# Loading the query weights and K first, and the gated unit's weights late, in a decode attention kernel

## The chip, the cores and the metric

The kernel runs on one core of a Trainium2 chip. The metric is device time in microseconds. The profile shows the engines PE (matrix products, with weight loads as PEld), DVE (vector), ACT (activations), POOL and SP, and 16 DMA engines that serve the queues of SP, ACT and POOL. In this kernel both SP and ACT issue the large loads, and ACT computes besides.

## The reference

One decoding step for 8 sequences with one token each. Two branches start from the normalized token and meet in a product.

```python
xn = _layernorm(x)                      # x: [8, 1, 512]
# branch A: attention over the last 2048 of 8192 cached keys; 32 query heads, 8 key heads, Dh 128
q = (xn @ wq)                           # wq: [512, 4096]
k = k_cache[:, :, Sk - W:, :]           # W = 2048, each key head serves 4 query heads
v = v_cache[:, :, Sk - W:, :]
p = softmax(q @ k.T * Dh ** -0.5)
s = (p @ v) @ wo                        # wo: [4096, 512]
# branch B: the gated unit
h = sigmoid(xn @ w_gate) * (xn @ w_up)  # [512, 1792] each
g = silu(h @ w_down)                    # w_down: [1792, 512]
out = x + s * g
```

All inputs are bf16. The windows of K and V are 32 MiB each, Wq and Wo 4 MiB each, the three weights of the gated unit 1.75 MiB each.

## The kernel before

**Tiles and the ring.** K and V are loaded in 16 tiles each of 2 MiB (one sequence, four of its eight key heads): K0 to K15 and V0 to V15. All large loads, weights too, go into a ring of 10 equal buffers (`ring_tile`, lines 90 and 91): a new tile takes the buffer of the tile ten allocations earlier, and its load waits until that one has been read. `free_bufs` counts in Python how many loads may be issued at a point of the program; `issue_loads` (line 133) issues from the sorted list `loads`. `load` (line 84) alternates between the queues of ACT and SP when no queue is given.

**Order of the start.** The program issues x, the three weights of the gated unit (`wg_sb`, `wu_sb`, `wd_sb`), the two halves of Wq, and then K and V as buffers allow. After the layer norm (lines 216 to 248) PE computes the gated unit (lines 251 to 285: 56 products with wg, 56 with wu, 28 with wd, to `gate`) and then the queries (`q_projection`, 128 products, and four copies into `qz_sb`).

**The slots.** The main loop (line 500) goes over slots t. A K or V tile is worked on in four slots. In slot t PE transposes a quarter of a K tile in two halves (`k_half`, line 321, each copied by DVE), multiplies the quarter of slot t - 1 with the queries (`qk`, line 335), and multiplies a quarter of V with the probabilities of slot u = t - 11 (`pv`, line 431). There are 64 such quarters, so t runs to 74. A batch takes eight slots. After a batch's scores its softmax is spread over slots by phase `ph` = t modulo 8: maximum at 0, `soft_exp` at 1 (a small product, a minimum, the exp on ACT, line 370), transposition and permutation at 2 (line 384 on DVE, line 390 on PE, copy on ACT at line 394), masks at 3 (line 402, DVE), denominators at 4 (`soft_den`, line 422). Each engine executes its own instructions in program order, DMA issues among them.

**The end.** Once all K and V loads are issued and seven buffers are free by count (slot 63), `load_wo` (line 458) issues Wo in seven pieces with a ring buffer each, four on SP and three on ACT. `o_rows(0)` and `o_rows(1)` turn the attention output around after the last slots of V, 64 products with Wo follow (line 541), then two DVE operations with `gate` and x, and two output DMAs. The PSUM buffer with the tag `misc` is single: the small product of `soft_exp`, the products with wd, the denominators and `o_rows` take turns in it.

Of the kernel before, what the change touches and what calls it, by code (L numbers as in the profile page):

```python
# [10 lines left out]
def kernel(  # L11
# [13 lines left out]
    nc = tc.nc  # L25
    P = 128
    B, _, D = A_x.shape
    _, Hkv, Sk, Dh = A_k_cache.shape
# [3 lines left out]
    F = B_w_gate.shape[1]  # L32
    KT = D // P
    FT = F // P
    win0 = Sk - W
    scale = float(Dh) ** -0.5
    HG = Hq // 4
# [7 lines left out]
    NJ = 4  # L45
# [4 lines left out]
    NT = B * NG  # L50
    SPB = NG * NJ
    NSLOT = B * SPB
    PV_LAG = SPB + 3
    QPAD = XR - rep
    RING = 10
    NCOL = 2
    DC = D // NCOL

    bf16 = mybir.dt.bfloat16
    f32 = mybir.dt.float32  # L60
    AF = mybir.ActivationFunctionType
    ALU = mybir.AluOpType
# [5 lines left out]
    work = ctx.enter_context(tc.tile_pool(name="work", bufs=1))  # L68
# [4 lines left out]
    psum = ctx.enter_context(  # L73
        tc.tile_pool(name="psum", bufs=2, space=bass.MemoryType.PSUM)
    )
    psum1 = ctx.enter_context(
        tc.tile_pool(name="psum1", bufs=1, space=bass.MemoryType.PSUM)
    )
# [5 lines left out]
    def load(dst, src, q=None):  # L84
        if q is None:
            q = queues[turn[0] % 2]
            turn[0] += 1
        q.dma_start(out=dst, in_=src)

    def ring_tile(shape, name):  # L90
        return ring.tile(shape, bf16, name=name, tag="ring", align_bytes=ALIGN)
# [1 line left out]
    x_bf = work.tile([B, D], bf16, name="x_bf")  # L93
    nc.sync.dma_start(out=x_bf[:], in_=A_x.flatten_outer_dims())

    wg_sb = ring_tile([P, KT, F], "wg_sb")
    wu_sb = ring_tile([P, KT, F], "wu_sb")
    wd_sb = ring_tile([P, FT, D], "wd_sb")
    load(wg_sb[:], B_w_gate.rearrange("(p kt) n -> p kt n", kt=KT), nc.scalar)
    load(wu_sb[:], B_w_up.rearrange("(p kt) n -> p kt n", kt=KT), nc.sync)  # L100
    load(wd_sb[:], B_w_down.rearrange("(p t) n -> p t n", t=FT), nc.sync)
    wq_view = A_wq.rearrange("(p kt) n -> p kt n", kt=KT)
    KH = KT // 2
    wq_sb = []
    for kh in range(2):
        t = ring_tile([P, KH, Hq * Dh], f"wq_sb{kh}")
        load(t[:], wq_view[:, kh * KH : (kh + 1) * KH, :], nc.scalar if kh == 0 else nc.sync)
        wq_sb.append(t)

    k_tiles = {}  # L110
    v_tiles = {}

    def load_kv(cache, i, name):
        b, gg = divmod(i, NG)
        t = ring_tile([P, CH, Dh], name)
        load(
            t[:].rearrange("p c d -> p (c d)"),
            cache[b, GL * gg : GL * (gg + 1), win0:Sk, :].rearrange(
                "j (p c) d -> p j (c d)", c=CH
            ),  # L120
        )
        return t

    loads = sorted(
        [(NJ * i, 0, i) for i in range(NT)]
        + [(NJ * i + PV_LAG, 1, i) for i in range(NT)]
    )
    loads_done = [0]  # L130
    free_bufs = [RING - 5]

    def issue_loads():
        while loads_done[0] < len(loads) and free_bufs[0] > 0:
            _, kind, i = loads[loads_done[0]]
            if kind:
                v_tiles[i] = load_kv(A_v_cache, i, "v_sb")
            else:
                k_tiles[i] = load_kv(A_k_cache, i, "k_sb")
            loads_done[0] += 1  # L140
            free_bufs[0] -= 1

# [3 lines left out]
    for j in range(NCOL):  # L146
        nc.gpsimd.dma_start(
            out=x2_sb[32 * j : 32 * j + B, :],
            in_=A_x.flatten_outer_dims()[:, DC * j : DC * (j + 1)],
# [7 lines left out]
    for off in range(-rep * (NJ - 1), rep * NJ, rep):  # L157
        nc.gpsimd.affine_select(
            out=SumM[:],
            in_=SumM[:],  # L160
# [9 lines left out]
        out=SumM_blk,  # L170
        in_=SumM_blk,
# [7 lines left out]
        out=SumM_blk,  # L179
        in_=SumM_blk,  # L180
# [11 lines left out]
        out=Jneg[:],  # L192
        in_=ident[:].rearrange("p (a j r) -> p j a r", j=NJ, r=rep),
        axis=AX.XY,
        op=ALU.add,
    )
    nc.vector.tensor_scalar(
        out=Jneg[:], in0=Jneg[:], scalar1=-scale, scalar2=None, op0=ALU.mult
# [4 lines left out]
        out=Hm[:],  # L203
        in_=ident[:].rearrange("p (a gl) -> p gl a", gl=GL),
        axis=AX.X,
        op=ALU.add,
# [4 lines left out]
        out=perm[:].rearrange("k (p gl) -> k p gl", gl=GL),  # L211
        in_=ident[:].rearrange("k (gl p) -> k p gl", gl=GL),
# [17 lines left out]
        out=rstd[:], in_=mv[:, 1:2], func=AF.Sqrt, bias=eps_t[:], scale=1.0  # L230
# [4 lines left out]
        out=xn_bf[:],  # L235
        in0=x_f[:],
# [6 lines left out]
    for kt in range(KT):  # L243
        nc.tensor.transpose(  # L244
            out=xnT_ps[:, kt, :], in_=xn_bf[:B, kt::KT], identity=ident[:B, :B]
# [2 lines left out]
    nc.vector.tensor_copy(out=xnT_sb[:], in_=xnT_ps[:])  # L248


    g_ps = psum.tile([P, FT, B], f32, name="g_ps", tag="s_ps")
    u_ps = psum.tile([P, FT, B], f32, name="u_ps", tag="s_ps")
    for w_sb, d_ps in ((wg_sb, g_ps), (wu_sb, u_ps)):
        for t in range(FT):
            for kt in range(KT):
                nc.tensor.matmul(
                    d_ps[:, t, :],
                    lhsT=w_sb[:, kt, t::FT],
                    rhs=xnT_sb[:, kt, :],
                    start=(kt == 0),  # L260
                    stop=(kt == KT - 1),
                )
    sig = work.tile([P, FT, B], f32, name="sig")
    nc.scalar.activation(out=sig[:], in_=g_ps[:], func=AF.Sigmoid)
    hT_sb = work.tile([P, FT, 32], bf16, name="hT_sb")
    nc.vector.memzero(hT_sb[:])
    nc.vector.tensor_tensor(
        out=hT_sb[:, :, :B], in0=sig[:], in1=u_ps[:], op=ALU.mult
    )
    b_ps = psum1.tile([NCOL * 32, DC], f32, name="b_ps", tag="misc")  # L270
    for t in range(FT):
        for j in range(NCOL):
            nc.tensor.matmul(
                b_ps[32 * j : 32 * (j + 1), :],
                lhsT=hT_sb[:, t, :],
                rhs=wd_sb[:, t, DC * j : DC * (j + 1)],
                start=(t == 0),
                stop=(t == FT - 1),
                tile_position=(0, 32 * j),
                skip_group_check=True,  # L280
            )
    sigb = work.tile([NCOL * 32, DC], f32, name="sigb")
    nc.scalar.activation(out=sigb[:], in_=b_ps[:], func=AF.Sigmoid)
    gate = work.tile([NCOL * 32, DC], f32, name="gate")
    nc.vector.tensor_tensor(out=gate[:], in0=sigb[:], in1=b_ps[:], op=ALU.mult)
    free_bufs[0] += 3
    issue_loads()


    def q_projection():  # L290
# [160 lines left out]
                op=ALU.mult,  # L451
            )


    wo_view = A_wo.rearrange("(hg p j) n -> p hg j n", p=P, j=4)
    wo_parts = {}

    def load_wo():
        for q, h0, h1, j0, j1 in (
            (nc.sync, 0, 2, 0, 4),  # L460
            (nc.scalar, 2, 4, 0, 4),
            (nc.sync, 4, 5, 0, 4),
            (nc.scalar, 5, 6, 0, 4),
            (nc.sync, 6, 7, 0, 4),
            (nc.scalar, 7, 8, 0, 2),
            (nc.sync, 7, 8, 2, 4),
        ):
            t = ring_tile([P, h1 - h0, j1 - j0, D], f"wo_sb{h0}{j0}")
            load(t[:], wo_view[:, h0:h1, j0:j1, :], q)
            for hg in range(h0, h1):  # L470
                for j in range(j0, j1):
                    wo_parts[hg, j] = t[:, hg - h0, j - j0, :]

    o2_sb = work.tile([P, HG, 4, 32], bf16, name="o2_sb")
    nc.vector.memzero(o2_sb[:])
    HGH = HG // NG
# [23 lines left out]
    for t in range(NSLOT + PV_LAG):  # L500
        u = t - PV_LAG
        b, ph = t // SPB - 1, t % SPB
        in_b = 0 <= b < B
        if t < NSLOT:
            k_half(t, 0)
        if in_b and ph == 3:
            soft_mask(b)
            dh_of[b] = soft_den_part(b)
        if t < NSLOT:
            k_half(t, 1)  # L510
        if in_b and ph == 2:
            soft_turn(b)
        if 0 <= t - 1 < NSLOT:
            qk(t - 1)
        if in_b and ph == 0:
            mj_of[b] = soft_max_part(b)
        if in_b and ph == 1:
            soft_exp(b, mj_of.pop(b))
        if u >= 0:
            pv(u)  # L520
        if in_b and ph == 2:
            soft_permute(b)
        if in_b and ph == 4:
            soft_den(b, dh_of.pop(b))
        if t < NSLOT and t % NJ == NJ - 1:
            free_bufs[0] += 1
        if u >= 0 and u % NJ == NJ - 1:
            free_bufs[0] += 1
        issue_loads()
        if loads_done[0] == len(loads) and not wo_parts and free_bufs[0] >= 7:  # L530
            load_wo()
        if u == NSLOT - NJ - 1:
            o_rows(0)
    o_rows(1)
# [4 lines left out]
    for n, (hg, j) in enumerate(order):  # L539
        for c in range(NCOL):  # L540
            nc.tensor.matmul(  # L541
                a_ps[32 * c : 32 * (c + 1), :],
                lhsT=o2_sb[:, hg, j, :],
                rhs=wo_parts[hg, j][:, DC * c : DC * (c + 1)],
                start=(n == 0),
                stop=(n == len(order) - 1),
                tile_position=(0, 32 * c),
                skip_group_check=True,
# [5 lines left out]
    for c in range(NCOL):  # L554
        queues[c].dma_start(
            out=out.flatten_outer_dims()[:, DC * c : DC * (c + 1)],
            in_=y_bf[32 * c : 32 * c + B, :],
# [31 lines left out]
```

## Time and profile before

| | |
|---|---|
| median of 3 runs | 206.28 us (205.15 to 206.87) |
| profiled execution, own time | 206.49 us |
| profiled execution, span | 204.4 us |
| PE busy | 158.1 us, 77% |
| PE weight loads | 117.0 us, 57% |
| DVE busy | 118.7 us, 58% |
| ACT busy | 15.7 us, 8% |
| DMA | 81.40 MB, mean 398 GB/s |
| chain that ended last | PE 43%, DMA 42%, DVE 11% |

The span goes from the first to the last instruction of the core; the execution's own time has some 2 us more around it. Times in views of the trace count from the start of the span. A timeline row has start, duration, engine, line, operation, output and input tile, shape and count; in brackets the idle time of the engine just before it and what ended that. PEclk is the granted share of PE's clock, in tenths. A row of ACTq or SPq is the issue of a DMA, not the transfer. A tile's name ends without its number, so `o_sb` stands for `o2_sb`, `x_sb` for `x2_sb`.

### The profile page before, as it was taken

What the parts mean: (1) busy time and instruction counts of PE and PEld (TensorE: products, weight loads), DVE (VectorE), ACT (ScalarE), POOL (GpSimd) and SP (SyncE); (2) the same over time, 40 slices, a digit from 0 to 9 for tenths busy, and PEclk for the clock granted to TensorE, in tenths of its full rate; (3) what the DMA queues carried; (4) which work ended last, traced back from release to release, by engine and by line L of the source; (5) the groups of instructions that cost most, each with busy time, mean ns of one, the idle gap of its engine ahead of it and who ended that gap; (6) DMA issues with size and microseconds to landing.
All of it is one profiled execution on the core that took longest, in us unless ns stands there. A gap on an engine that the chain in (4) does not pass through costs nothing.

```text
span 204.4 us, 5925 instructions
## 1 busy us (share of the span) xinstructions
PE 158.1 (77%) x2712; PEld 117.0 (57%) x2712; DVE 118.7 (58%) x248; ACT 15.7 (8%) x30; POOL 7.4 (4%) x20
## 2 busy tenths in 40 slices
PE   0003971999988997999899799988798996993893
PEld 0003941866656765676676577665666674662862
DVE  2402010367888687776868777686468767664311
ACT  0005000002020011002001100200020002002000
POOL 7600000000000000000000000000000000000000
PEclk9999997559999999999999999999799999997558
DMA  6999999999999999999999999999999999999700
GB/s 209 437 430 433 425 436 420 433 430 430 439 414 431 430 430 433 420 430 430 426 436 420 430 433 423 438 417 433 430 420 439 423 433 425 420 426 407 288 24 2
DMA packets 6728, 81.40 MB, mean 398 GB/s; under 512 B 776, under 2 KB 816, under 8 KB 1968
## 3 DMA queue, kind: packets, MB, share of 16 engines
q1 hardware_dynamic: 3472, 41.69, 47.9%
q10 hardware_dynamic: 3168, 39.33, 45.6%
q8 instruction: 21, 0.34, 0.6%
q14 instruction: 3, 0.02, 0.0%
q0 software_dynamic: 64, 0.01, 0.0%
HBM read 81.02 MB, written 0.01 MB: 396 GB/s over the span
## 4 chain that ended last, share of the span: by engine, by line
PE 43%; DMA 42%; DVE 11%; issue 1%; ACT 1%; SPq 1%; ACTq 0%
DMA v_sb<-in_A_v_cache_dram 19%; PE kT_ps L328 18%; DMA wq_sb<-in_A_wq_dram 16%; PE oT_ps L439 9%; PE s_ps L344 8%; DMA wo_sb<-in_A_wo_dram 7%; DVE kT_sb L331 5%; PE a_ps L541 3%; DVE pT_sb L402 3%; DVE pt_bf L384 2%; PE qT_ps L294 2%; PE pT_ps L390 1%; PE mb_ps L365 1%; PE den_ps L424 1%; DVE qz_sb L302 1%
## 5 line engine op out<-in xcount | busy, mean ns | idle before, releaser
L331 DVE COPY kT_sb<-kT_ps 128x1024 bf16<-128x1024 bf16 x128 | 83.3, 686 | 31.8 <-PE kT_ps L328 31.2
L328 PE MATMUL kT_ps<-ident,k_sb 128*128 128x128 bf16 x1024 | 71.4, 225 | 0.7 <-DVE kT_sb L331 0.7
L328 PEld LDWEIGHTS <-k_sb 128*128 128x128 bf16 x1024 | 62.3, 101 | 9.8 <-issue 8.8
L439 PEld LDWEIGHTS <-v_sb 128*128 128x128 bf16 x1024 | 31.1, 98 | 34.4 <-issue 26.3
L439 PE MATMUL oT_ps<-pT_sb,v_sb 128*128 128x16 bf16 x1024 | 34.9, 170 | 11.1 <-DVE pT_sb L402 6.8
L344 PE MATMUL s_ps<-kT_sb,qz_sb 128*32 128x512 bf16 x256 | 39.7, 610 | 0.0
L244 PE MATMUL xnT_ps<-ident,xn_bf 8*128 8x8 bf16 x4 | 0.3, 174 | 18.6 <-DVE xn_bf L234 18.6
L370 ACT ACTIVATE p_bf<-s_ps,nm 128x512 bf16<-128x512 f32 x8 | 5.5, 687 | 111.6 <-DVE nm L367 98.4
L244 PEld LDWEIGHTS <-xn_bf 8*128 8x128 bf16 x4 | 0.2, 114 | 18.5 <-DVE xn_bf L234 18.5
L344 PEld LDWEIGHTS <-qz_sb 128*32 128x32 bf16 x256 | 6.6, 93 | 6.9 <-issue 0.8
L402 DVE TENSOR_SCALAR pT_sb<-pc_bf,Hm 128x512 bf16<-128x512 bf16 x32 | 9.1, 346 | 1.2 <-ACT pc_bf L394 1.2
L294 PE MATMUL qT_ps<-xnT_sb,wq_sb 128*128 128x8 bf16 x128 | 3.7, 168 | 5.6 <-DMA wq_sb<-in_A_wq_dram 4.6
L294 PEld LDWEIGHTS <-wq_sb 128*128 128x128 bf16 x128 | 3.6, 104 | 6.0 <-DMA wq_sb<-in_A_wq_dram 4.7
L390 PE MATMUL pT_ps<-pt_bf,perm 128*128 128x512 bf16 x8 | 3.2, 402 | 5.0 <-DVE pt_bf L384 5.0
L541 PE MATMUL a_ps<-wo_sb,o_sb 128*32 128x256 bf16 x64 | 6.6, 386 | 0.2 <-issue 0.2
L232 DVE RECIPROCAL rstd<-rstd 8x1 f32<-8x1 f32 x1 | 0.1, 150 | 10.4 <-ACT rstd L229 10.4
L302 DVE CAST qz_sb<-qT_ps 128x64 bf16<-128x64 f32 x4 | 1.3, 586 | 8.4 <-PE qT_ps L294 8.4
L384 DVE STREAM_TRANSPOSE pt_bf<-p_bf 128x512 bf16<-128x512 bf16 x8 | 5.6, 702 | 0.9 <-ACT p_bf L370 0.9
L394 ACT CAST pc_bf<-pT_ps 128x512 bf16<-128x512 f32 x8 | 4.7, 586 | 16.3 <-PE pT_ps L390 16.3
L356 DVE TENSOR_REDUCE mx<-s_ps 128x1 f32<-128x512 f32 x8 | 5.5, 682 | 0.8 <-PE s_ps L344 0.8
L541 PEld LDWEIGHTS <-o_sb 128*32 128x32 bf16 x64 | 4.5, 136 | 2.0 <-issue 0.7
L426 DVE RECIPROCAL rden<-den_ps 128x32 f32<-128x32 f32 x8 | 2.9, 358 | 4.5 <-PE den_ps L424 4.5
(55 smaller groups left out, 62.6 us busy)
## 6 DMA issues: line engine op xcount, KB each, us to landing
k_sb<-in_A_k_cache_dram ACTq DMA_DIRECT2D x15, 2048.0 KB, 30.4
v_sb<-in_A_v_cache_dram SPq DMA_DIRECT2D x15, 2048.0 KB, 39.4
wq_sb<-in_A_wq_dram ACTq DMA_DIRECT2D x1, 2048.0 KB, 17.8
wq_sb<-in_A_wq_dram SPq DMA_DIRECT2D x1, 2048.0 KB
k_sb<-in_A_k_cache_dram SPq DMA_DIRECT2D x1, 2048.0 KB, 41.7
v_sb<-in_A_v_cache_dram ACTq DMA_DIRECT2D x1, 2048.0 KB, 36.3
wg_sb<-in_B_w_gate_dram ACTq DMA_DIRECT2D x1, 1792.0 KB, 9.1
wu_sb<-in_B_w_up_dram SPq DMA_DIRECT2D x1, 1792.0 KB, 14.3
```

The source lines that it names most:

```text
L294: nc.tensor.matmul(qT_ps[:, h * B : (h + 1) * B], lhsT=wq_sb[kt // KH][:, kt % KH, h * Dh : (h + 1) * Dh], rhs=xnT_sb[:, kt, :], start=(kt ...
L328: nc.tensor.transpose(out=kT_ps[:, jj, :], in_=k_sb[:, c0 + jj, :], identity=ident[:, :])
L331: nc.vector.tensor_copy(out=kT_tiles[t][:, h2 * HALF : (h2 + 1) * HALF, :], in_=kT_ps[:])
L344: nc.tensor.matmul(s_tiles[b][XR * gl : XR * (gl + 1), :], lhsT=qz_sb[:, b, GL * gg + gl, z0 : z0 + XR], rhs=kT[:, :, gl::GL], start=(x == 0),
L356: nc.vector.reduce_max(out=mx[:], in_=s_tiles[b][:], axis=AX.X)
L370: nc.scalar.activation(out=p_bf[:], in_=s_tiles.pop(b)[:], func=AF.Exp, bias=nm[:], scale=scale, accum_out=den128[:],)
L384: nc.vector.transpose(out=pt_bf[:], in_=p_bf[:])
L390: nc.tensor.matmul(pT_ps[:], lhsT=perm[:], rhs=pt_tiles.pop(b)[:], start=True, stop=True)
L394: nc.scalar.copy(out=pc_bf[:], in_=pT_ps[:])
L402: nc.vector.tensor_scalar(out=pT_tiles[b][:, :, gl].rearrange("p c x r -> p c (x r)"), in0=pc, scalar1=Hm[:, gl : gl + 1], scalar2=None, o ...
L439: nc.tensor.matmul(o_tiles[b][:, GW * gg : GW * (gg + 1)], lhsT=v_sb[:, CC * j + cc, :], rhs=pT_tiles[b][:, cc, :, x, :], start=(j == 0 an ...
L541: nc.tensor.matmul(a_ps[32 * c : 32 * (c + 1), :], lhsT=o2_sb[:, hg, j, :], rhs=wo_parts[hg, j][:, DC * c : DC * (c + 1)], start=(n == 0), ...
```

## The change

Wq's two halves become the first large loads, followed by K and V. The three weights of the gated unit come after K15 and V13, ahead of V14 and V15. Its products and activations move into the main loop: those with wg and wu, both with the multiply into `hT_sb`, to the end of slot 66 (behind the last batch's permutation), those with wd and `gate` to the end of slot 67. Their two PSUM tiles now use the tag `kT_ps`. Wo comes last, in two ring buffers of which the first is loaded by two DMAs and the second by five; they are part of the list of loads and so are issued when a buffer is counted free (slots 58 and 59). Queues alternate for all loads but the last piece of Wo, which goes to SP. All arithmetic stays as it was.

```diff
-    wg_sb = ring_tile([P, KT, F], "wg_sb")
-    wu_sb = ring_tile([P, KT, F], "wu_sb")
-    wd_sb = ring_tile([P, FT, D], "wd_sb")
-    load(wg_sb[:], B_w_gate.rearrange("(p kt) n -> p kt n", kt=KT), nc.scalar)
-    load(wu_sb[:], B_w_up.rearrange("(p kt) n -> p kt n", kt=KT), nc.sync)
-    load(wd_sb[:], B_w_down.rearrange("(p t) n -> p t n", t=FT), nc.sync)
...
-        load(t[:], wq_view[:, kh * KH : (kh + 1) * KH, :], nc.scalar if kh == 0 else nc.sync)
+        load(t[:], wq_view[:, kh * KH : (kh + 1) * KH, :])
...
+    def load_mlp(kind):
+        if kind == 2:
+            t = ring_tile([P, FT, D], "wd_sb")
+            load(t[:], B_w_down.rearrange("(p t) n -> p t n", t=FT))
+            wd_sb.append(t)
+        else:
+            t = ring_tile([P, KT, F], ("wg_sb", "wu_sb")[kind])
+            load(t[:], (B_w_gate, B_w_up)[kind].rearrange("(p kt) n -> p kt n", kt=KT))
+            (wg_sb, wu_sb)[kind].append(t)
...
+    loads[-2:-2] = [(2, 0), (2, 1), (2, 2)]
+    loads += [(3, 0), (3, 1)]
     loads_done = [0]
-    free_bufs = [RING - 5]
+    free_bufs = [RING - 2]
...
+    def load_wo(half):
+        t = ring_tile([P, HG // 2, 4, D], f"wo_sb{half}")
+        for h0, h1, j0, j1 in (
+            ((0, 2, 0, 4), (2, 4, 0, 4)),
+            ((4, 5, 0, 4), (5, 6, 0, 4), (6, 7, 0, 4), (7, 8, 0, 2), (7, 8, 2, 4)),
+        )[half]:
+            q = nc.sync if (h0, j0) == (7, 2) else None
+            o = half * (HG // 2)
+            load(t[:, h0 - o : h1 - o, j0:j1, :], wo_view[:, h0:h1, j0:j1, :], q)
...
-    g_ps = psum.tile([P, FT, B], f32, name="g_ps", tag="s_ps")
-    u_ps = psum.tile([P, FT, B], f32, name="u_ps", tag="s_ps")
-    for w_sb, d_ps in ((wg_sb, g_ps), (wu_sb, u_ps)):
+    def unit_in(w_sb):
+        d_ps = psum.tile([P, FT, B], f32, name="d_ps", tag="kT_ps")
...
+    def unit_mid():
+        g_ps, u_ps = d_tiles
+        sig = work.tile([P, FT, B], f32, name="sig")
+        nc.scalar.activation(out=sig[:], in_=g_ps[:], func=AF.Sigmoid)
+        nc.vector.tensor_tensor(
+            out=hT_sb[:, :, :B], in0=sig[:], in1=u_ps[:], op=ALU.mult
+        )
+
+    def unit_out():
+        b_ps = psum1.tile([NCOL * 32, DC], f32, name="b_ps", tag="misc")
...
-        if loads_done[0] == len(loads) and not wo_parts and free_bufs[0] >= 7:
-            load_wo()
+        if t == NSLOT + 2:
+            unit_in(wg_sb[0])
+            unit_in(wu_sb[0])
+            unit_mid()
+            free_bufs[0] += 2
+            issue_loads()
+        if t == NSLOT + 3:
+            unit_out()
+            free_bufs[0] += 1
+            issue_loads()
```

More of the change, by code (lines that the diff above doesn't have):

```diff
@@ L122, in load_kv @@
         return t
[L126 to L129, printed above, removed]
-    loads_done = [0]
-    free_bufs = [RING - 5]
+    wg_sb = []
+    wu_sb = []
+    wd_sb = []
+    def load_mlp(kind):
[7 more added lines that the diff above has]
+            (wg_sb, wu_sb)[kind].append(t)
+    loads = [
+        (kind, i)
+        for _, kind, i in sorted(
+            [(NJ * i, 0, i) for i in range(NT)]
+            + [(NJ * i + PV_LAG, 1, i) for i in range(NT)]
+        )
+    ]
+    loads[-2:-2] = [(2, 0), (2, 1), (2, 2)]
+    loads += [(3, 0), (3, 1)]
+    loads_done = [0]
+    free_bufs = [RING - 2]
+    wo_view = A_wo.rearrange("(hg p j) n -> p hg j n", p=P, j=4)
+    wo_parts = {}
+    def load_wo(half):
[7 more added lines that the diff above has]
+            load(t[:, h0 - o : h1 - o, j0:j1, :], wo_view[:, h0:h1, j0:j1, :], q)
+            for hg in range(h0, h1):
+                for j in range(j0, j1):
+                    wo_parts[hg, j] = t[:, hg - o, j, :]
     def issue_loads():
         while loads_done[0] < len(loads) and free_bufs[0] > 0:
-            _, kind, i = loads[loads_done[0]]
-            if kind:
+            kind, i = loads[loads_done[0]]
+            if kind == 0:
+                k_tiles[i] = load_kv(A_k_cache, i, "k_sb")
+            elif kind == 1:
                 v_tiles[i] = load_kv(A_v_cache, i, "v_sb")
+            elif kind == 2:
+                load_mlp(i)
             else:
-                k_tiles[i] = load_kv(A_k_cache, i, "k_sb")
+                load_wo(i)
             loads_done[0] += 1
@@ L248 @@
     nc.vector.tensor_copy(out=xnT_sb[:], in_=xnT_ps[:])
-    g_ps = psum.tile([P, FT, B], f32, name="g_ps", tag="s_ps")
-    u_ps = psum.tile([P, FT, B], f32, name="u_ps", tag="s_ps")
-    for w_sb, d_ps in ((wg_sb, g_ps), (wu_sb, u_ps)):
+    d_tiles = []
+    hT_sb = work.tile([P, FT, 32], bf16, name="hT_sb")
+    nc.vector.memzero(hT_sb[:])
+    gate = work.tile([NCOL * 32, DC], f32, name="gate")
+    def unit_in(w_sb):
+        d_ps = psum.tile([P, FT, B], f32, name="d_ps", tag="kT_ps")
         for t in range(FT):
@@ L262 @@
                 )
[L263 to L287, printed above, removed]
+        d_tiles.append(d_ps)
+    def unit_mid():
[4 more added lines that the diff above has]
+            out=hT_sb[:, :, :B], in0=sig[:], in1=u_ps[:], op=ALU.mult
+        )
+    def unit_out():
+        b_ps = psum1.tile([NCOL * 32, DC], f32, name="b_ps", tag="misc")
+        for t in range(FT):
+            for j in range(NCOL):
+                nc.tensor.matmul(
+                    b_ps[32 * j : 32 * (j + 1), :],
+                    lhsT=hT_sb[:, t, :],
+                    rhs=wd_sb[0][:, t, DC * j : DC * (j + 1)],
+                    start=(t == 0),
+                    stop=(t == FT - 1),
+                    tile_position=(0, 32 * j),
+                    skip_group_check=True,
+                )
+        sigb = work.tile([NCOL * 32, DC], f32, name="sigb")
+        nc.scalar.activation(out=sigb[:], in_=b_ps[:], func=AF.Sigmoid)
+        nc.vector.tensor_tensor(out=gate[:], in0=sigb[:], in1=b_ps[:], op=ALU.mult)
     def q_projection():
@@ L452, in pv @@
             )
[L455 to L472, printed above, removed]
     o2_sb = work.tile([P, HG, 4, 32], bf16, name="o2_sb")
```

## The prediction

> **What bounds the kernel now.** First I read the slices of the page.
>
> ```profile
> PE   0003971999988997999899799988798996993893
> PEclk9999997559999999999999999999799999997558
> DMA  6999999999999999999999999999999999999700
> ```
>
> The transfers are at 9 tenths or more from the second slice to the 37th. The stages (busy time by window) give 421 to 439 GB/s in every stretch from 5 to 180 us. PE is idle for three slices and has holes later. So the middle of the kernel is paced by 81.0 MB of loads, and a step that only makes PE start earlier buys nothing there. What remains is the end: which wait ends last. The timeline of the end:
>
> ```profile
> 185.12 0.69 ACT L370 ACTIVATE p_bf<-s_ps,nm 128x512 bf16<-128x512 f32 x1 [13.23 <-DMA wo_sb<-in_A_wo_dram]
> 186.69 0.58 PE L390 MATMUL pT_ps<-pt_bf,perm 128*128 128x512 bf16 x1 [1.07 <-DVE pt_bf L384]
> 187.93 1.14 DVE L402 TENSOR_SCALAR pT_sb<-pc_bf,Hm 128x512 bf16<-128x512 bf16 x4 [1.23 <-ACT pc_bf L394]
> 189.13 1.00 PE L439 MATMUL oT_ps<-pT_sb,v_sb 128*128 128x16 bf16 x32 [1.85 <-DVE pT_sb L402]
> 189.98 0.61 PE L424 MATMUL den_ps<-dh,ones 128*128 128x32 f32 x2
> 191.99 1.88 PE L439 MATMUL oT_ps<-pT_sb,v_sb 128*128 128x16 bf16 x64
> 195.46 5.55 PE L541 MATMUL a_ps<-wo_sb,o_sb 128*32 128x256 bf16 x57 [0.19 <-issue]
> ```
>
> The reader sees a chain on PE: softmax of the last batch (exp 185.12, permutation 186.69 to 187.27, masks 187.93), the last eight slots of products with V (189.13 to 193.87), Wo, output. From the end of the last product with V to the end of the span it is 204.4 - 193.87 = 10.5 us. Behind V12's products (PE waited for that tile until 174.24) came nine slots, so V12 started this chain.
>
> Then the issues, for what waits for what.
>
> ```profile
> 162.85 0.34 SPq L88 DMA_DIRECT2D wo_sb<-in_A_wo_dram  x1
> SPq L88 <- DMA k_sb<-in_A_k_cache_dram: 4.1, 1, 4.1
> 172.19 0.33 SPq L88 DMA_DIRECT2D wo_sb<-in_A_wo_dram  x1
> SPq L88 <- DMA v_sb<-in_A_v_cache_dram: 5.4, 1, 5.4
> 174.22 0.35 ACTq L88 DMA_DIRECT2D wo_sb<-in_A_wo_dram  x1
> 181.76 0.36 ACTq L88 DMA_DIRECT2D wo_sb<-in_A_wo_dram  x1
> ```
>
> Counted in program order over both queues, every issue waits until the load eight issues before it has landed: SP's piece of 172.19 waited for K15 (162.85 + 0.34 + 4.1: landed 167.3), its next piece for V14 (172.19 + 0.33 + 5.4: 177.9), ACT's piece of 174.22 for V12 (174.2), that of 181.76 for V13 (181.7). An ACT that waits to issue computes nothing: here the exp of the last batch, which stands behind these issues in program order, was free at 182.1 and lost nothing, since its input came at 185.0.
>
> **The change part by part.**
>
> *Wq and K first.* Before, PE waited for Wq's second half until 35.25 and began K at 38.6. Now Wq leads each queue. Scaled from the rows of before (the first 1.84 MB on SP landed at 15.6), the second half lands near 17 and K starts near 21. Price on the path: 0, some 18 us earlier start or not, because transfers set the pace. PE needs 17.8 us for a batch (oT at 62.6 to 80.4), the transfers 4 x 2.097 MB / 0.429 = 19.6 us, so PE will now catch up and wait for each tile. If the cover fails (PE behind the loads at the end) the early start is what makes it good, so no loss here.
>
> *Where loads land.* K stays on ACT's queue and V on SP's. On ACT 37.48 MB had landed with V14 at 177.9 and 35.39 MB with K15 at 167.3. Now wg completes 35.39 MB there: 167.3; wd 37.22 MB: 177.9 - 0.26 / 2.10 x 10.6 = **176.6**. K15 (33.55 MB, before K14 33.29 at 157.7) comes at 158.9. On SP, 35.13 MB had landed with V12 at 174.2, at some 4.9 us a MB: V13 (33.55 MB) 166.6, wu (35.39) 175.5, V14 (37.49) 185.4. V15, on ACT behind wd, some 186. The sum of bytes is the same, so the last piece of Wo comes, as before (181.82 + 13.8), near 195.6.
>
> *Wo in two buffers.* Its seven issues move from slot 63 to slots 58 and 59, ahead of the last exp (slot 65). ACT's three wait, by the rule of eight, for K15, wg and **wd**. So ACT stands until 176.6 and issues 0.42 us more. Behind it are queued: exp of batch 7, its copy, both sigmoids; PE's permutation waits for the exp, and all PE work of slots 66 to 74 for the permutation. Without this wait the exp would run at 166.6 + 0.5 + 2.4 = 169.5 (2.4 from the last scores at 182.75 to the exp at 185.12). On SP the same rule makes the last piece wait for V14 (185.4); nothing computes there.
>
> *The gated unit at slots 66 and 67.* Its rows from the start of the kernel:
>
> ```profile
> 19.11 3.47 PE L256 MATMUL g_ps<-xnT_sb,wg_sb 128*128 128x8 bf16 x56 [0.27 <-DVE xnT_sb L248]
> 22.43 3.50 PE L256 MATMUL u_ps<-xnT_sb,wu_sb 128*128 128x8 bf16 x56
> 26.04 0.27 DVE L267 TENSOR_TENSOR hT_sb<-sig,u_ps 128x112 bf16<-128x112 f32 x1 [6.74 <-PE u_ps L256]
> 26.36 3.15 PE L273 MATMUL b_ps<-wd_sb,hT_sb 128*32 128x256 bf16 x28 [0.42 <-DVE hT_sb L267]
> 29.55 0.38 ACT L283 ACTIVATE sigb<-b_ps 64x256 f32<-64x256 f32 x1 [6.68 <-PE b_ps L273]
> 29.96 0.41 DVE L285 TENSOR_TENSOR gate<-sigb,b_ps 64x256 f32<-64x256 f32 x1 [3.66 <-ACT sigb L283]
> ```
>
> Before they were hidden under the wait for Wq. Now they stand in PE's order behind the last permutation and ahead of the last products with V. The multiply into hT is also ahead of the masks in DVE's order, so the masks wait for all 112 products. The sigmoid's table load (1.28 us) lies under the second 56.
>
> *The sum.* ACT free 176.6 + 0.42 = 177.0, the exp; permutation done 2.15 later (185.12 to 187.27): 179.2. To hT's end 7.20 (19.11 to 26.31): 186.4. Masks and start of V's slot 56, 1.20 (187.93 to 189.13): 187.6. That slot, half of 1.00: 188.1. Products with wd 3.15: 191.25. The denominators use the PSUM buffer of these products and wait for the gate, 0.92 (29.51 to PE's next at 30.43, slot 57 under it): 192.2. Denominators 0.47 (chain: 190.13 to 190.60): 192.65. To the last product with V 3.28 (190.59 to 193.87): 195.95. To the end 10.5: span **206.45**. The profiled execution took 206.49 for a span of 204.4, so 2.1 lie outside: **208.5**, against its own 206.49 and the runs' median of 206.28, 1.0 to 1.1% more. Against before: the last exp comes 8.1 us earlier (177.0 for 185.12), because K and V are through earlier, and the unit puts 7.20 - 0.66 (the copy that ran there) + 3.15 + 0.4 = 10.1 behind it.
>
> The clock of the tail isn't shown by before and is bounded from both sides. PE idles from about 169.5 to 179.2, and the unit's own rows came after 18 us of idling, so they hold for it (the record of the granted clock begins at 29.4; before that the windows print 1.00, but the products with wd took 421 ns, median, as those with Wo did at 0.50). For the 64 products with Wo the cold row is 421 ns (median), the last of them, after the clock was back, 272 ns: 64 take 6.7 us or 6.7 x 272 / 421 = 4.3. I take the cold one, since the granted clock stayed at 0.50 from 187 to 200 while PE was busy for 0.73 to 1.00 of nearly every us from 189.
>
> The Trainium skill (TensorE: Matmul & The Clock Gate, Part 1) says that an idle window of about 3.4 us halves the array's clock and about 3.4 us of sustained work restores it. It speaks against a change that opens 9 us of idling before the tail, but then it would have the clock back soon after 183, and the sum would be 2.4 lower, 206.1. The trace of before disagrees on the second half: over 10 us of nearly busy PE, the first half of it thin products with 16 moving columns, didn't restore it.
>
> **Rivals.**
>
> A, *not slower*: the wait for wd doesn't hold the exp (the place: ACT's third Wo issue in slot 59). Then the exp runs at 169.5, hT is done at 179, and V14 decides: slot 56 at 185.4, then 0.5 + 3.15 + 0.92 + 0.47 + 3.28 + 10.5: span 204.2, time 206.3; with V14 3 us earlier, 203.4. It takes over from any hold that ends before 174.6. For it: ACT's issues here cost the exp nothing. Against: the waits of 174.22 and 181.76 are of just this kind.
>
> B: the tail runs at full clock: 208.5 - 2.4 = 206.1. For it: the 28 wide products with wd end 5 us before Wo's, and the clock did come back at 29.4, at the end of such products. Against: it fell again 3.4 us later (32.9), and here the products with Wo start 5 us later.
>
> C: ACT's queue now becomes the late one (it carries 41.2 MB, SP 39.9; before 39.3 and 41.7). SP's 37.2 MB landed at 181.7, 5.1 us behind ACT's: wd at 181.7 gives 213.6, and half of that 211. Against: SP was late from its first load on, before byte counts could tell.
>
> D: the change doesn't do what it says, so that the unit isn't in a gap at all. That is the forecast itself.
>
> **How the numbers follow.** Forecast 0.50, own range 206.8 to 210.3 (1.5 us either way for wd's landing); A 0.12; B 0.20; C 0.18. The predicted time is the forecast's, 208.5. The range reaches to A and B together or with an earlier V14 (204.6) and to the middle of C (211.6). A change of 1% is about what a measurement of this kernel can tell from none; 1% above 206.28 is 208.3, 1% below 204.2. Slower: 0.30 of the forecast, 0.17 of C, 0.03 of B: 0.50. Same: 0.20, 0.01, 0.15 of B, 0.05 of A: 0.41. Faster: 0.07 of A, 0.02 of B: 0.09.
>
> **What would show it.** K's products begin near 21 us; PE has holes before each tile in the middle, DMA still full. ACT issues its last piece of Wo near 176.6 and the last exp follows at once, at 177; the last products with wd end near 191, with V near 196, the span near 206.5. If the last exp comes near 170, A holds; if the products with Wo take under 5 us, B; if ACT's last issue is past 179, C. The prediction is wrong at the root if the loads end well off 195 or PE is still behind them at slot 60.

## The result and the profile after

The changed kernel took **213.5 us** (median of 4 runs, 212.68 to 214.12) against 205.92 us for the kernel before (median of 4 runs beside it): ratio 1.036, 95% interval 1.030 to 1.043. The direction was forecast, the size was not: 208.5 had been predicted and 211.6 was the upper end of the range. The profiled execution took 214.12 us for a span of 212.1.

The same three lines of the profile, each with the span in 40 slices:

```profile
PE   0017999699989789795999797989779810097893
PEclk9999999999999999999699999999999955555858
DMA  6999999999999999999999999999999999993000
```

PE is in its main loop earlier (K from 20.4 instead of 38.6), DMA is as full as before, and the loads are over at the same time (slice 37, some 196 us). What is new is the hole in PE in slices 33 to 35 while DMA is still full. The timeline of the end:

```profile
169.52 0.97 PE L477 MATMUL oT_ps<-pT_sb,v_sb 128*128 128x16 bf16 x32
183.85 0.69 ACT L408 ACTIVATE p_bf<-s_ps,nm 128x512 bf16<-128x512 f32 x1 [26.41 <-DMA v_sb<-in_A_v_cache_dram]
185.42 0.58 PE L428 MATMUL pT_ps<-pt_bf,perm 128*128 128x512 bf16 x1 [14.94 <-DVE pt_bf L422]
185.80 3.50 PE L293 MATMUL d_ps<-xnT_sb,wg_sb 128*128 128x8 bf16 x56
189.16 3.50 PE L293 MATMUL d_ps<-xnT_sb,wu_sb 128*128 128x8 bf16 x56
192.77 0.27 DVE L306 TENSOR_TENSOR hT_sb<-sig,d_ps 128x112 bf16<-128x112 f32 x1 [7.34 <-PE d_ps L293]
194.15 0.58 PE L477 MATMUL oT_ps<-pT_sb,v_sb 128*128 128x16 bf16 x16 [1.48 <-DVE pT_sb L440]
194.66 2.97 PE L314 MATMUL b_ps<-wd_sb,hT_sb 128*32 128x256 bf16 x28
198.55 0.41 PE L462 MATMUL den_ps<-dh,ones 128*128 128x32 f32 x2 [0.43 <-DVE gate L325]
200.29 1.84 PE L477 MATMUL oT_ps<-pT_sb,v_sb 128*128 128x16 bf16 x64
202.58 6.06 PE L567 MATMUL a_ps<-wo_sb,o_sb 128*32 128x256 bf16 x63
```

PE has nothing from 170.5 to 185.4: it waits for the permutation's input, and that for the exp. The exp's minimum was ready at 169.86 (L405 ends then), yet the exp starts at 183.85, and its row says what ACT waited for: a V tile, which the exp itself doesn't read. In the chain of waits the whole stretch is one piece:

```profile
146.31 37.08 DMA v_sb<-in_A_v_cache_dram
183.39 0.02 issue
183.41 0.34 ACTq L88
...
183.85 0.79 ACT p_bf L408 x2
```

It is ACT's last issue of Wo that waits, until V14 has landed. ACT's last two issues:

```profile
174.06 0.35 ACTq L88 DMA_DIRECT2D wo_sb<-in_A_wo_dram  x1
183.41 0.34 ACTq L88 DMA_DIRECT2D wo_sb<-in_A_wo_dram  x1
```

So the mechanism is the forecast one, an issue of Wo that holds the exp behind it; but the tile that was waited for is another, 183.4 and not 176.6.

**Which issue waits for which.** In this program the loads on both queues share eight completion counters that go round, and an issue waits until the previous load on its counter has landed. I had counted in the order of the program text. In the built program the issues of Wo's second buffer, and with them the counters, come in another order, as its listing shows (hg is the index h0 of a piece in `load_wo`; 7 is loaded in two parts, a and b):

```
          before                        changed kernel
piece     queue  waits for landing of   queue  waits for landing of
hg 4      SP     K14                    SP     V13
hg 5      ACT    V12                    ACT    wu    (counted: wg)
hg 6      SP     K15                    SP     wg    (counted: wu)
hg 7, a   ACT    V13                    ACT    V14   (counted: wd)
hg 7, b   SP     V14                    SP     wd    (counted: V14)
```

The trace agrees. What SP's issues of hg 6 and of 7, b waited for, from the waits of SP's queue, each with the issue that followed:

```profile
SPq L88 <- DMA wg_sb<-in_B_w_gate_dram: 3.8, 1, 3.8
169.73 0.33 SPq L88 DMA_DIRECT2D wo_sb<-in_A_wo_dram  x1
SPq L88 <- DMA wd_sb<-in_B_w_down_dram: 8.5, 1, 8.5
178.55 0.33 SPq L88 DMA_DIRECT2D wo_sb<-in_A_wo_dram  x1
```

Before, the order of the text and that of the counters agree, so that trace could not show the difference.

### The profile page after: what moved, and what is told of

Its sections match the earlier page's. It is cut to its first block, busy times and chain, and to the rows that moved or that the text cites. A ratio compares the mean times of both kernels' runs of the same rounds, so it can differ in the third digit from the quotient of the medians.

```text
span 212.1 us, 5924 instructions
## 1 busy us (share of the span) xinstructions
PE 156.8 (74%) x2712; PEld 116.8 (55%) x2712; DVE 118.4 (56%) x248; ACT 15.7 (7%) x30; POOL 7.6 (4%) x20
## 4 chain that ended last, share of the span: by engine, by line
DMA 77%; PE 15%; DVE 3%; ACTq 1%; issue 1%; ACT 1%; DVEq 0%
DMA k_sb<-in_A_k_cache_dram 60%; DMA v_sb<-in_A_v_cache_dram 17%; PE d_ps L293 3%; PE oT_ps L477 3%; PE a_ps L567 3%; PE kT_ps L366 3%; PE b_ps L314 1%; PE s_ps L382 1%; ACTq L88 1%; DVE pT_sb L440 1%; DVE kT_sb L369 1%; DVE pt_bf L422 1%; PE pT_ps L428 0%; ACT p_bf L408 0%; PE o_ps L500 0%
## 5 line engine op out<-in xcount | busy, mean ns | idle before, releaser
L366 PE MATMUL kT_ps<-ident,k_sb 128*128 128x128 bf16 x1024 | 69.9, 223 | 9.1 <-DMA k_sb<-in_A_k_cache_dram 9.1
L366 PEld LDWEIGHTS <-k_sb 128*128 128x128 bf16 x1024 | 61.1, 100 | 18.8 <-DMA k_sb<-in_A_k_cache_dram 9.8
L293 PEld LDWEIGHTS <-wg_sb 128*128 128x128 bf16 x56 | 3.6, 161 | 15.2 <-issue 15.2
L567 PE MATMUL a_ps<-wo_sb,o_sb 128*32 128x256 bf16 x64 | 6.1, 379 | 0.0
L567 PEld LDWEIGHTS <-o_sb 128*32 128x32 bf16 x64 | 5.2, 135 | 0.6
```

The lines of the kernel that those rows point to most:

```text
L293: nc.tensor.matmul(d_ps[:, t, :], lhsT=w_sb[:, kt, t::FT], rhs=xnT_sb[:, kt, :], start=(kt == 0), stop=(kt == KT - 1),)
L366: nc.tensor.transpose(out=kT_ps[:, jj, :], in_=k_sb[:, c0 + jj, :], identity=ident[:, :])
L567: nc.tensor.matmul(a_ps[32 * c : 32 * (c + 1), :], lhsT=o2_sb[:, hg, j, :], rhs=wo_parts[hg, j][:, DC * c : DC * (c + 1)], start=(n == 0), ...
```

## The experiments

The theory after the result: ACT's last issue of Wo sets the exp's start, and everything behind the exp follows at fixed distances, until the landing of V14 and V15 takes over. Rivals: the unit's place on PE is the cost by itself, or the bytes on the queues are. Each time is a median over rounds beside the kernel before on the same chip (205.83 to 206.08 us in the three comparisons).

**1. All of Wo on SP's queue.**

```diff
-            q = nc.sync if (h0, j0) == (7, 2) else None
+            q = nc.sync
```

> All seven pieces of Wo on SP's queue, nothing else changed; so ACT has no issue ahead of the last exp. Theory (the hold of ACT sets the end): the last exp comes near 170 instead of 183.85, the unit's products run in PE's idle time from 172 to 179, and V14's landing (183.4) decides: V slot 56 at 183.5 and then 17.95 us as in the changed kernel (194.15 to 212.1), span 201.5, time about 203.3. Rival (the unit's place behind the last permutation is the cost, whatever ACT does): over 210. Rival (Wo's last bytes are the end): SP then ends later and the time stays above 206.

Measured 204.05 us, ratio 0.991 (0.988 to 0.995). With this one line the change is 0.9% faster than the kernel before instead of 3.6% slower. The timeline of its end:

```profile
170.11 0.69 ACT L408 ACTIVATE p_bf<-s_ps,nm 128x512 bf16<-128x512 f32 x1 [12.52 <-DVE nm L405]
175.24 3.50 PE L293 MATMUL d_ps<-xnT_sb,wu_sb 128*128 128x8 bf16 x56
183.41 0.59 PE L477 MATMUL oT_ps<-pT_sb,v_sb 128*128 128x16 bf16 x16 [4.68 <-DMA v_sb<-in_A_v_cache_dram]
183.94 3.11 PE L314 MATMUL b_ps<-wd_sb,hT_sb 128*32 128x256 bf16 x28
```

The exp runs when its input is there, the 112 products are done at 178.7, and now the first V slot waits for V14, as the theory has it.

**2 and 3. Doses of the hold.** In 2 ACT's last piece goes to SP, which leaves ACT's earlier wait for wu. In 3 the pieces hg 4 and hg 5 become one on SP and hg 6 goes to ACT: one issue fewer, which moves ACT's last piece to the counter of wd, with the same bytes on each queue.

```diff
-            q = nc.sync if (h0, j0) == (7, 2) else None
+            q = nc.sync if h0 == 7 else None                    # 2
```

```diff
-            ((4, 5, 0, 4), (5, 6, 0, 4), (6, 7, 0, 4), (7, 8, 0, 2), (7, 8, 2, 4)),
+            ((4, 6, 0, 4), (6, 7, 0, 4), (7, 8, 0, 2), (7, 8, 2, 4)),   # 3: SP, ACT, ACT, SP
...
-            q = nc.sync if (h0, j0) == (7, 2) else None
+            q = nc.sync if (h0, j0) in ((4, 0), (7, 2)) else nc.scalar if half else None
```

> The quarter-megabyte piece of Wo that ACT issued last goes to SP, so that ACT's last issue waits for wu (174.1) instead of V14 (183.4). Theory of the hold: exp near 174.6, everything after it as before, so 9.2 us earlier than in the changed kernel: span 202.9, time about 204.3. Rival (place of the unit alone): unchanged, 213.

> Wo's second half in four pieces (two of SP's merged), with the same bytes on each queue, so that ACT's last issue waits for wd (178.5). It is the wait of the prediction. Theory of the hold: exp at 179.0, 4.85 us earlier than in the changed kernel: span 207.3, time about 208.6. If only the removal of the whole hold counts or the hold doesn't count: 213.

Measured 205.72 us for 2, ratio 0.999 (0.996 to 1.002), and 208.53 us for 3, ratio 1.015 (1.010 to 1.021). The exp's row in each, 2 first:

```profile
174.28 0.69 ACT L408 ACTIVATE p_bf<-s_ps,nm 128x512 bf16<-128x512 f32 x1 [16.76 <-DMA wu_sb<-in_B_w_up_dram]
```

```profile
178.76 0.69 ACT L408 ACTIVATE p_bf<-s_ps,nm 128x512 bf16<-128x512 f32 x1 [21.45 <-DMA v_sb<-in_A_v_cache_dram]
```

The name in brackets in 3 is the profile's guess; the issue ahead of it was freed at 178.3, the landing of wd. With the exp at 170.1 (run 1), 174.3, 178.8 and 183.85 (the changed kernel) the first slot of V14 starts at 183.4, 184.6, 189.1 and 194.15: in run 1 it waits for V14, in the other three it comes 10.3 us after the exp. The spans are 202.1, 203.0, 205.9 and 212.1. They follow less evenly, because from the last product with V to the end it takes 10.5, 9.9, 8.7 and 10.0 us, with the products with Wo at different granted clocks. The place of the unit was the same in all four, so it is not the cost by itself.

**4. No gated unit.** The unit's 140 products and its activations are left out, the gate is a constant, the loads stay.

```diff
-            unit_in(wg_sb[0])
-            unit_in(wu_sb[0])
-            unit_mid()
...
-            unit_out()
+            nc.vector.memset(gate[:], 0.5)
```

> The gated unit's 140 products and activations are left out (its weights are still loaded, the gate is a constant). ACT's issues of Wo stay and its last still waits for V14. By the sum of the prediction the unit puts 6.5 + 3.6 = 10.1 us behind the last exp: span 202.0, time 203.4. If the hold alone were the cost and the unit hidden: 213. If the exp is not near 183.9, the reading of the hold is wrong.

Measured 207.63 us, ratio 1.009 (1.005 to 1.012), and the exp at 187.6. The expectation failed, and the run says nothing on the unit's price: without readers of the three weights, the load of wd in the built program also waits for the landing of wg. It was issued at 168.25 instead of 140.0, and the last quarter of K was transposed at 183.23 instead of 165.6:

```profile
168.25 0.33 ACTq L88 DMA_DIRECT2D wd_sb<-in_B_w_down_dram  x1
171.07 0.69 ACT L408 ACTIVATE p_bf<-s_ps,nm 128x512 bf16<-128x512 f32 x1 [31.91 <-DMA wu_sb<-in_B_w_up_dram]
```

It shows the same hold in another place. The second row is the exp of the batch before the last: its minimum was ready at 153.8, but ACT stood at its issues of wd and then of V15 (170.42), so it ran at 171.07, and PE was idle from 156.0 to 172.6.

**5 and 6. A thin unit, held and free.** To keep the loads and their waits in place, the unit is cut to 8 products with wg and wu and 2 with wd (130 are left out), with two copies for the sigmoid and the multiply. Run 5 is otherwise the changed kernel, run 6 has Wo on SP as in 1.

```diff
-        for t in range(FT):
+        for t in range(1):
...
-        nc.scalar.activation(out=sig[:], in_=g_ps[:], func=AF.Sigmoid)
-        nc.vector.tensor_tensor(
-            out=hT_sb[:, :, :B], in0=sig[:], in1=u_ps[:], op=ALU.mult
-        )
+        nc.vector.tensor_copy(out=hT_sb[:, 0, :B], in_=g_ps[:, 0, :])
+        nc.vector.tensor_copy(out=hT_sb[:, 1, :B], in_=u_ps[:, 0, :])
```

> The changed kernel with the gated unit cut to 8 + 2 of its 140 products and two copies in the place of sigmoid and multiply (130 products left out; all loads, all their places and ACT's issues stay). Earlier kernel without a unit moved the loads, this one should not: ACT's last issue still at 183.4, exp at 183.85. By the prediction's terms the first V slot comes at 188.1 instead of 194.15 and 2.9 us of products with wd go: span 203.1, time about 204.6. If the unit were hidden: 213.5.

> The same thin unit, with all of Wo on SP's queue, so that ACT holds nothing. V14 (183.4) and V15 (186.4) decide, then Wo's last piece (195.7): last product with V near 188.3, products with Wo until 196.2, 3.5 us to the end: span 199.7, time 201.8. Against the whole unit with Wo on SP (204.05) that puts the unit's price without the hold at 2.3 us; if the two prices simply added, it would be the 9 us that the thin unit saves under the hold.

Measured 205.38 us (ratio 0.998, 0.996 to 1.001) and 201.5 us (0.980, 0.977 to 0.984); the exps at 183.76 and 170.95. The four corners, in us:

| | whole unit | thin unit | price of the unit |
|---|---|---|---|
| ACT held until V14 | 213.5 | 205.38 | 8.1 |
| ACT not held | 204.05 | 201.5 | 2.55 |
| price of the hold | 9.45 | 3.9 | |

The corners come from two comparisons, in which the kernel before differs by 0.16 us. The prices don't add, as the theory says: without the hold the 112 products lie in PE's wait for V14, with it they stand behind. In run 6 another bound is reached, the loads themselves. Its chain of waits ends with the last piece of Wo and four products:

```profile
183.24 12.35 DMA wo_sb<-in_A_wo_dram
195.58 0.04 issue
195.62 0.41 PE a_ps L564 x4
```

So 2.55 us is what the unit costs above this bound, which less work on PE does not lower.

**7. The products with wd earlier.** Wo on SP, and the products with wd directly behind the multiply.

```diff
             unit_mid()
-            free_bufs[0] += 2
-            issue_loads()
-        if t == NSLOT + 3:
             unit_out()
-            free_bufs[0] += 1
+            free_bufs[0] += 3
             issue_loads()
```

> Wo on SP's queue and the 28 products with wd directly behind the multiply in slot 66, ahead of V slot 56. They then run in PE's wait for V14 (hT ready near 179, wd landed at 178.5). Theory: the unit is hidden whole, span 199.7 as without it, time 201.8, 2% under before. If the products with wd are not what lies between V14 and the end: 204 as with Wo on SP alone.

Measured **202.71 us**, ratio 0.986 (0.981 to 0.991): the fastest kernel here with the whole computation, 1.3 us faster than 1 and 1.2 slower than the thin unit, so not hidden whole.

```profile
178.92 3.17 PE L314 MATMUL b_ps<-wd_sb,hT_sb 128*32 128x256 bf16 x28 [0.43 <-DVE hT_sb L306]
182.88 1.13 DVE L440 TENSOR_SCALAR pT_sb<-pc_bf,Hm 128x512 bf16<-128x512 bf16 x4
184.06 0.94 PE L477 MATMUL oT_ps<-pT_sb,v_sb 128*128 128x16 bf16 x32 [1.97 <-DVE pT_sb L440]
```

In DVE's order the masks now stand behind the gate, and the first V slot waits for them until 184.06 instead of for V14 (183.3). That is not where the time is lost, though: the last product with V ends at 188.5, before run 6's (189.0). Behind it the products with Wo run from 190.5 to 196.6, at a granted clock of 0.50 until about 196, and the span is 199.9, 0.5 more than run 6's 199.4. The remaining difference of the medians is not in this profile: the four executions took 201.87, 202.04, 203.37 and 203.38 us, and the profiled one is of the shorter pair.

**8. The start alone.** The kernel before with Wq and K first; the unit's weights lie between V0 and K3 and its products in slot 11.

```diff
+        + [(NJ * 3 - 0.5, 2, i) for i in range(3)]
...
+        if t == NJ * 3 - 1:
+            unit()
```

> The kernel before with only the start changed: Wq and K first, the gated unit's weights between V0 and K3 with its products in slot 11, Wo in seven buffers at slot 63 as before. K starts near 20 instead of 38.6. Prediction's claim (the early start is worth nothing because transfers set the pace, and V12 landing near 174 sets the tail): same as before, 205.9 within 1. Rival (the early start saves PE time that reaches the end): under 203.

Measured 205.62 us, ratio 0.997 (0.994 to 1.001): no difference. PE starts K at 22.3 instead of 38.6, and the last stretch of the chain begins with V12, as the prediction read it for the kernel before:

```profile
133.15 40.27 DMA v_sb<-in_A_v_cache_dram
173.43 0.05 issue
173.47 0.56 PE oT_ps L450 x16
```

**9. ACT's issues later, on ACT.** The queues as in the changed kernel, ACT's three issues of Wo behind the first sigmoid.

```diff
             unit_mid()
+            for part in later:          # the three pieces of ACT
+                load(*part)
```

> The changed kernel with its queues as they are, but ACT's three issues of Wo stand behind the first sigmoid in ACT's program order (slot 66) and no longer ahead of the last exp. If the gain of Wo on SP alone came from ACT's order, this one gives the same: last exp near 170, V14 decides, span 201.5 to 202.5, time 203.5 to 204.5 (the second sigmoid now waits for ACT's issue at 183.8, before the products with wd end). If it came from the bytes that moved to the other queue: 213.

Measured 204.65 us, ratio 0.994 (0.992 to 0.997); the exp at 169.93. The bytes stayed on their queues and the gain is there all the same, so it is ACT's program order.

## Why the prediction was right and wrong

*The step that failed*: "ACT's three wait, by the rule of eight, for K15, wg and **wd**". That an issue waits eight loads back held; that the loads count in the order of the program text did not. The term "ACT free 176.6 + 0.42 = 177.0" measured 183.85. Of these 6.85 us, 1.9 are wd's landing (178.5 in the changed kernel, 176.6 predicted) and 4.9 are V14 (183.4) in its place. Run 3 restores the predicted wait and gives 208.53, the predicted 208.5; but that is partly luck, since there wd is 1.7 later (178.3) and the tail behind the exp is 27.1 (178.76 to 205.9) instead of the 29.45 of the sum.

*The tail behind the exp* measured 28.25 us (183.85 to 212.1), 1.2 less than the sum: hT ended 9.19 after the exp began (sum 9.4), V slot 56 started 1.11 later (1.20), the last product with V ended at 202.13, 7.98 later (8.35), and from there the end took 10.0 (10.5). So 206.45 + 6.85 - 1.2 = 212.1.

*Where loads land* held within 2.5 us: wg came at 169.7 (predicted 167.3), wu at 174.0 (175.5), wd at 178.5 (176.6), V14 at 183.4 (185.4), and the loads were over near 196.

*Wq and K first, price 0*: right, by run 8. K started at 20.4 (predicted near 21).

*The unit's price*, 10.1 us behind the exp: the thin unit gives 8.1 of it back under the hold (213.5 to 205.38), with 10 products and the masks still there. Right in kind.

*Rival A* did not come true in the changed kernel, where the hold was there and longer than forecast. What it says of a kernel without the hold is run 1: V14 decides. Its 206.3 came out as 204.05, because V14 landed 2.0 earlier than worked out; from V14 to the end it is 18.7 us (183.4 to 202.1), 18.8 in the rival's sum. *Rival B* came true in part: the clock does come back behind the products with wd, falls again, and in run 3 is full once more under the products with Wo. The windows of run 3:

```profile
192.00:194.00 2.00, 1.60 (x30) 1.04 (x27) 0.41 (x1) 0.38 (x1) 0.00 (x0) 0.72 0.48 192
194.00:196.00 2.00, 1.73 (x73) 1.71 (x71) 0.99 (x3) 0.00 (x0) 0.00 (x0) 1.00 0.15 50
...
200.00:202.00 2.00, 2.00 (x40) 2.00 (x38) 0.00 (x0) 0.00 (x0) 0.00 (x0) 1.00 0.00 0
```

After the start and end of the window the columns are PE, PEld, DVE, ACT and POOL, each busy time with its count, then the granted clock. It is full from about 193 to 196.6 and again from 200, and the products with Wo run at 20 a us there instead of 11 to 13 in the changed kernel. *Rival C*'s mark (ACT's last issue past 179) came true for another reason: ACT's queue was not late, wd landed at 178.5 and not at 181.7.

*The bounds of the range* don't all follow from their sums: A and B together give 206.3 - 2.4 = 203.9 and not 204.6, the middle of C is 211.1 and not 211.6, and 1.5 us either way is 207.0 to 210.0.

## What to carry to other kernels

An engine that computes and issues DMAs has its program order as a hidden dependency: whatever load the issue waits for, all its later arithmetic waits for too, so look at which landing frees the last issue ahead of a critical instruction, in the built program and not in the text. Moving work to a place where an engine idles only pays if the instruction that opens this place isn't itself held; price the two together, because here 8.1 us under the hold were 2.55 without it. And where transfers set the pace, an early start is worth nothing (run 8), while work behind the last wait is worth most of its time (8.1 of the unit's 10.1 us in run 5).

## What the runs showed of the hardware that was not expected

PE's clock. In the changed kernel PE is busy with the 112 thin products (8 moving columns) from 185.8 to 192.6, and the granted clock is 0.50 all the way; it is full for about 3.4 us only after the 2.97 us of products with wd (256 columns):

```profile
188.00:190.00 2.00, 2.00 (x36) 2.00 (x36) 0.00 (x0) 0.26 (x1) 0.00 (x0) 0.50 1.03 419
196.00:198.00 2.00, 2.00 (x34) 1.41 (x30) 0.00 (x0) 0.33 (x1) 0.00 (x0) 0.68 0.00 0
198.00:200.00 2.00, 1.31 (x39) 1.23 (x36) 0.94 (x3) 0.05 (x1) 0.00 (x0) 1.00 0.03 8
```

Run 1 shows the other direction. There the same products begin at 171.9 with the clock still full, PE has been idle for no stretch above 1.1 us since 165, and the clock falls under them, at about 173.2:

```profile
172.00:174.00 2.00, 2.00 (x37) 2.00 (x36) 0.00 (x0) 1.87 (x2) 0.00 (x0) 0.80 0.94 402
174.00:176.00 2.00, 2.00 (x36) 2.00 (x36) 0.00 (x0) 0.26 (x1) 0.00 (x0) 0.50 1.03 442
```

The Trainium skill (TensorE: Matmul & The Clock Gate, Part 1) puts the warm-up at some 3.4 us of sustained work, whatever the number of matmuls. By these rows 6.8 us of busy PE did not restore the clock, nor keep it, and 3 us did; that the width of the products makes the difference fits, but no run here varied it alone. Nor are 3 us always enough: in run 2 the products with wd (185.09 to 188.26) leave the clock at 0.50, and it is full only from about 197.4, under the products with Wo:

```profile
188.00:189.00 1.00, 0.78 (x20) 0.50 (x16) 0.29 (x1) 0.38 (x1) 0.00 (x0) 0.50 1.01 414
197.00:198.00 1.00, 1.00 (x20) 0.83 (x16) 0.00 (x0) 0.00 (x0) 0.00 (x0) 0.80 0.00 0
```

The timing may explain that. In the changed kernel the clock changes at about 170.0, 197.3, 200.7 and 207.5, some 8, 1 and 2 times 3.4 us apart. Laid on steps of 3.4 us, the products with wd fill 2.6 us of the step that ends with the clock's return, and in run 2 (steps counted back from 197.4) no more than 2.1 us of any. This is an estimate from the rows of the windows, not tested by a run.
